# Decay tables by ScalarE's DMA queue, state matmuls on quarter arrays, and tiles that agree modulo 512 bytes, in an attention and two-FFN kernel

## The chip, the core and the metric

One core of one Trainium2 chip runs the whole program. The metric is the device time of one execution in microseconds. The kernel before took 598.75 us (median of 3 runs, 598.46 to 598.89).

## What is computed

Attention with a decay per head, over 2 batches, 8 heads, 768 positions and 64 features a head, then two feed-forward layers on the 1536 tokens (512 to 2048 to 512, the first with x*tanh(softplus(x)), the second with x*clip(x+3,0,6)/6).

```python
Dmask = np.where(rel >= 0, lam[:, None, None] ** rel[None, :, :], 0.0)
intra = np.einsum('bhic,bhjc->bhij', qb, kb) * Dmask[None]
intra = np.einsum('bhij,bhjd->bhid', intra, vb)
inter = np.einsum('bhid,bhde->bhie', qb * lam_pow[None], kv_state)
out[:, :, sl] = intra + inter
kv_state = lam_block * kv_state + np.einsum('bhsd,bhse->bhde', kb * rev_pow[None], vb)
x = moe(attn_out); return moe2(x)
```

## The kernel before

**Attention** works on 12 chunks `c` of 128 positions, 6 for each batch; a chunk holds all 8 heads as 4 pairs `p` of two halves `h2`, with head `2p+h2` on partitions `h2*64` to `h2*64+63`. `load_raw` brings a chunk's q, k, k and v in two halves of 512 KB. `scores` (L148) makes two PSUM tiles `sc`, `weigh` (L163) multiplies them on VectorE by the mask into `amat` (L179) and, in the first four chunks, decays k and q on GpSimd (L170, L172). `attend` (L181) makes `u`, the chunk's addition to the state (L191, only where `carries(c)`), and accumulates in one PSUM bank `o` first 8 matmuls from `amat` (L197), all four pairs of half 0 and then all of half 1, and then, where `follows(c)`, 4 matmuls from `state` (L203). `state` is 128x128 for a pair, with zeros off the diagonal. `settle` (L210) adds `u` to the state on VectorE (L218), splits `o` into a high part on ScalarE and a low part on VectorE in `X`, and scales the state for the next chunk on ScalarE (L226). Of an f32 matmul the profile counts two instructions.

**The two layers** are 96 steps `n` in the list `seq`: each is 12 matmuls `h` (L274) from a weight tile `W[t]` and a token block `X[k]`, and 12 matmuls `y` (L287) from the activation `g` and the same weight tile. The list runs six passes over the upper tiles W8 to W15: one in group "split", two in "add", three in "out"; W0 to W7 have six too.

**Start.** `decay_tables` (L114) loads 8 numbers, makes 128 powers of each on 8 partitions (L126), writes them to DRAM (`z`, L131), and reads them back as the mask (L135) and, spread over all partitions, as `lampow` in `table` (L141). All of its DMAs are on SP's queue, in written order with the loads of `raw` and of the weights' stages `st` around it. The first `h` matmul needs the `X` of chunks 0 to 3, so these come before the layers; chunks 4 to 11 stand between the steps 0 to 15, where `att_at` puts them. Below that, a scheduler orders each engine's instructions.

**Where tiles lie.** Every partition's memory is filled from both ends. From the lower end X, W0 to W11 and g begin at byte 128 modulo 512. From the upper end come the pools tm2 (8192 bytes), tm1 (`pw`, 264 numbers, 1056 bytes), stage, and then at1 and raw; when attention ends, the pool "late" (L488) puts W12 to W15 in the place of the last two. The pools from stage on begin at 448 modulo 512, W12 to W15 among them.

Of the kernel before, what the change touches and what calls it, by code (L numbers as in the profile page):

```python
# [7 lines left out]
F32 = mybir.dt.float32  # L8
# [6 lines left out]
ACTF = mybir.ActivationFunctionType  # L15
ALU = mybir.AluOpType
# [5 lines left out]
def decay_attention__mish_ffn__hswish_ffn_kernel(  # L22
# [8 lines left out]
    nc = tc.nc  # L31
# [10 lines left out]
    tm2_p = ctx.enter_context(tc.tile_pool(name="tm2", bufs=2, side="right"))  # L42
    tm1_p = ctx.enter_context(tc.tile_pool(name="tm1", bufs=1, side="right"))
# [16 lines left out]
    at1 = att_stack.enter_context(tc.tile_pool(name="at1", bufs=1, side="right"))  # L60
# [5 lines left out]
    def split_hi(hi, src):  # L66
        nc.scalar.activation(out=hi, in_=src, func=ACTF.Copy)  # L67

    def split_lo(lo, hi, src):
        nc.vector.tensor_tensor(out=lo, in0=src, in1=f32(hi), op=ALU.subtract)  # L70

    z = dram_p.tile([8, 256], F32, name="z")
    mask = at1.tile([128, 2, 4, 128], F32, name="mask")
    state = [at1.tile([128, 4, 128], F32, name=f"state{i}") for i in range(2)]
    amat = [at1.tile([128, 4, 128], F32, name=f"amat{i}") for i in range(2)]
    table = at1.tile([128, 2, 512], F32, name="table")
    lampow = table[:, 0].rearrange("p (a i) -> p a i", a=4)
# [13 lines left out]
    def load_raw(c, i):  # L91
        if c >= NCH:
            return
        if i == 0:
            pool = lent_p if c in (2, 3) else raw_p
            raw_t[c] = pool.tile([128, 2048], F32, tag="raw", name="raw")
        s = slice(i * 1024, (i + 1) * 1024)
        ins = nc.sync.dma_start(out=raw_t[c][:, s], in_=att[c, :, s])
        if pinned[0]:
            tc.keep_in_program_order(ins)  # L100

    def qk(c):
        t = raw_t[c]
        return (t[:, i:i + 512].rearrange("p (a i) -> p a i", a=4) for i in (512, 0))

    def kv(c):
        t = raw_t[c]
        return t[:, 1024:1536], t[:, 1536:2048]
# [3 lines left out]
        return rr.to_broadcast([128, 4, 2, 64])  # L112

    def decay_tables():  # L114
        lam_sb = tm2_p.tile([128, 512], F32, tag="x", name="lam_sb")[0:8, 0:1]
        pw = tm1_p.tile([128, 264], F32, tag="th", name="pw")[0:8, 0:256]
        nc.sync.dma_start(out=lam_sb, in_=lam.unsqueeze(1))
        load_raw(0, 0)
        load_raw(0, 1)
        load_raw(1, 0)  # L120
        nc.vector.memset(pw[:, 0:127], 0.0)
        nc.vector.memset(pw[:, 127:128], 1.0)
        nc.vector.tensor_copy(pw[:, 128:129], lam_sb)
        m = 1
        while m < 128:
            nc.vector.tensor_scalar(  # L126
                out=pw[:, 128 + m:128 + 2 * m], in0=pw[:, 128:128 + m],
                scalar1=pw[:, 127 + m:128 + m], scalar2=None, op0=ALU.mult,
            )
            m *= 2  # L130
        tc.keep_in_program_order(nc.sync.dma_start(out=z, in_=pw))  # L131
        load_raw(1, 1)
        for h2 in range(2):
            base = z[h2:h2 + 1, 0:1]
            tc.keep_in_program_order(nc.sync.dma_start(  # L135
                out=mask[:, h2],
                in_=bass.AP(base.tensor, base.offset, [[1, 128], [512, 4], [1, 128]]),
            ))
        for h2 in range(2):
            base = z[h2:h2 + 1, 128:129]  # L140
            tc.keep_in_program_order(nc.sync.dma_start(  # L141
                out=lampow[h2 * 64:(h2 + 1) * 64],
                in_=bass.AP(base.tensor, base.offset, [[0, 64], [512, 4], [1, 128]]),
            ))
        for i in range(2):
            nc.gpsimd.memset(state[i], 0.0)

    def scores(c, pool, tag):  # L148
        qT, kT = qk(c)
# [7 lines left out]
    def carries(c):  # L157
        return c % CPB < CPB - 1

    def follows(c):  # L160
        return c % CPB > 0
# [19 lines left out]
    def attend(c, pool, tag):  # L181
        qT, kT = qk(c)
        kn, vn = kv(c)
        u = None
        if carries(c):
            u = ps_a.tile([128, 4, 128], F32, tag="at", name="u")
            for p in range(4):
                for h2 in range(2):
                    s = slice(p * 128 + h2 * 64, p * 128 + h2 * 64 + 64)
                    r = slice(h2 * 64, h2 * 64 + 64)  # L190
                    nc.tensor.matmul(u[r, p, r], lhsT=kn[:, s], rhs=vn[:, s], start=True, stop=True)  # L191
        o = pool.tile([128, 4, 128], F32, tag=tag, name="o")
        last = not follows(c)
        for h2 in range(2):
            for p in range(4):
                h = 2 * p + h2
                nc.tensor.matmul(  # L197
                    o[h2 * 64:h2 * 64 + 64, p, :], lhsT=vn[:, h * 64:h * 64 + 64], rhs=amat[h2][:, p, :],
                    start=(p == 0), stop=(last and p == 3), skip_group_check=True,
                )  # L200
        if follows(c):
            for p in range(4):
                nc.tensor.matmul(  # L203
                    o[:, p, :], lhsT=state[c % 2][:, p, :], rhs=qT[:, p, :],
                    start=False, stop=(p == 3), skip_group_check=True,
                )
        uo_t[c] = u, o
        del raw_t[c]

    def settle(c):  # L210
        u, o = uo_t.pop(c)
        off = (c % 4) * 128
        if carries(c):
            for h2 in range(2):
                r = slice(h2 * 64, h2 * 64 + 64)
                new = state[(c + 1) % 2][r, :, r]
                if follows(c):
                    nc.vector.tensor_tensor(out=new, in0=new, in1=u[r, :, r], op=ALU.add)  # L218
                else:
                    nc.vector.tensor_copy(new, u[r, :, r])  # L220
        hi = X[c // 4][:, 0, :, off:off + 128]
        split_hi(hi, o)
        split_lo(X[c // 4][:, 1, :, off:off + 128], hi, o)
        if carries(c) and carries(c + 1):
            for p in range(4):
                nc.scalar.activation(  # L226
                    out=state[c % 2][:, p, :], in_=state[(c + 1) % 2][:, p, :], func=ACTF.Copy,
                    scale=lampow[:, p, 127:128],
                )

    stage_t = {}

# [170 lines left out]
    nc.scalar.preload_act_table_set("mish")  # L403
    warm_up(10)
    decay_tables()
    load_raw(2, 0)
    load_w(*plan[0])
# [7 lines left out]
    for c in range(4):  # L415
        attend(c, ps_h, "h")
        if c == 0:
            load_raw(4, 0)
            load_w(*plan[2])
            load_raw(4, 1)  # L420
            load_w(*plan[3])
        if c == 1:
            load_raw(5, 0)
            load_raw(5, 1)
            pinned[0] = False
        if c < 3:
            weigh(c + 1)
        else:
            nc.gpsimd.tensor_copy(table[:, 1].rearrange("j (p h d) -> j p h d", p=4, h=2), reverse())
        if c < 2:  # L430
            scores(c + 2, ps_y, "y")
        settle(c)
        if c == 2:
            advance(1)
# [15 lines left out]
    for n in range(STEPS + 2):  # L450
# [12 lines left out]
        for kind in kinds:  # L463
            c = chunk[kind]
            if kind == "s":
                scores(c, ps_a, "at")
                weigh(c)
            else:
                attend(c, ps_a, "at")
                if len(kinds) > 1:  # L470
                    settle(c)
            chunk[kind] += 1
# [7 lines left out]
        if "o" in kinds:  # L480
            c = chunk["o"] - 1
            if len(kinds) == 1:
                settle(c)
            load_raw(c + 2, 0)
            load_raw(c + 2, 1)
            if c == NCH - 1:
                att_stack.close()
                pool = ctx.enter_context(tc.tile_pool(name="late", bufs=1, side="right", reuse_waits="tile"))  # L488
                for i in range(NF - NLATE, NF):
                    W[i] = pool.tile([128, 2, 1024], F32R, name=f"W{i}")  # L490
# [57 lines left out]
```

## Time and profile before

| | |
|---|---|
| median of 3 runs | 598.75 us |
| the profiled execution | 598.68 us |
| its span, first to last instruction | 596.8 us |
| TensorE (PE) busy | 585.1 us, 98% |
| VectorE (DVE) / ScalarE (ACT) busy | 276.6 / 255.9 us |
| PE waits that the profile puts down to another engine or a DMA | 7.8 us |

The profile is of one execution. PE busy is an overlap of pipelined matmuls, so PE's pace is read from the distance between starts: where 12 matmuls of one line are a row of the timeline, the distance to the next row's start is what they took. A "chain" follows the last instruction back through what released it.

### The profile page before, as it was taken

What the parts mean: (1) busy time and instruction counts of PE and PEld (TensorE: products, weight loads), DVE (VectorE), ACT (ScalarE), POOL (GpSimd) and SP (SyncE); (2) the same over time, 40 slices, a digit from 0 to 9 for tenths busy, and PEclk for the clock granted to TensorE, in tenths of its full rate; (3) what the DMA queues carried; (4) which work ended last, traced back from release to release, by engine and by line L of the source; (5) the groups of instructions that cost most, each with busy time, mean ns of one, the idle gap of its engine ahead of it and who ended that gap; (6) DMA issues with size and microseconds to landing.
All of it is one profiled execution on the core that took longest, in us unless ns stands there. A gap on an engine that the chain in (4) does not pass through costs nothing.

```text
span 596.8 us, 7263 instructions
## 1 busy us (share of the span) xinstructions
PE 585.1 (98%) x2938; PEld 477.2 (80%) x2938; DVE 276.6 (46%) x410; ACT 255.9 (43%) x440; POOL 9.7 (2%) x14
## 2 busy tenths in 40 slices
PE   5999999999999999999999999999999999999997
PEld 3877788888888888888888888888888888888885
DVE  2898886733656665510666872222222222222220
ACT  0577767513766666522466652222312222322222
POOL 1400000000000000000000000000000000000000
PEclk9999999999999999999999999999999999999999
DMA  7948744401343343200243220000100000100001
GB/s 228 406 174 290 246 156 142 141 1 71 107 142 116 131 134 113 71 2 0 71 141 113 97 73 1 1 2 0 71 0 1 0 1 0 71 0 1 0 1 70
DMA packets 15952, 50.53 MB, mean 85 GB/s; under 512 B 1576, under 2 KB 3120, under 8 KB 15920
## 3 DMA queue, kind: packets, MB, share of 16 engines
q1 hardware_dynamic: 15920, 50.08, 24.5%
q8 instruction: 23, 0.38, 0.3%
q14 instruction: 9, 0.07, 0.0%
HBM read 46.92 MB, written 3.15 MB: 84 GB/s over the span
## 4 chain that ended last, share of the span: by engine, by line
PE 95%; DVE 2%; DMA 2%; ACT 1%; issue 0%; ACTq 0%; DVEq 0%
PE h L274 44%; PE y L287 44%; PE o L197 3%; PE sc L154 2%; PE o L203 2%; PE u L191 1%; DMA z<-pw 1%; DMA mask<-z 1%; DVE st L255 0%; DVE amat L179 0%; DVE pw L126 0%; DMA lam_sb<-lam 0%; DVE W L70 0%; DVE st L258 0%; ACT W L67 0%
## 5 line engine op out<-in xcount | busy, mean ns | idle before, releaser
L274 PE MATMUL h<-X,W 128*128 128x512 f32 x1152 | 281.4, 393 | 0.0
L274 PEld LDWEIGHTS h<-X,W 128*128 128x128 f32 x1152 | 215.1, 188 | 47.5
L287 PE MATMUL y<-g,W 128*128 128x512 f32 x576 | 139.7, 391 | 0.0
L287 PE MATMUL y<-W,g 128*128 128x512 f32 x576 | 138.9, 391 | 0.0
L287 PEld LDWEIGHTS y<-g,W 128*128 128x128 f32 x576 | 108.0, 188 | 23.8 <-ACT W L67 0.3
L287 PEld LDWEIGHTS y<-W,g 128*128 128x128 f32 x576 | 108.2, 188 | 23.4
L70 DVE TENSOR_TENSOR g<-x,g 128x512 fp32r<-128x512 f32 x96 | 66.2, 691 | 78.9 <-ACT g L310 49.3
L320 DVE SCALAR_TENSOR_TENSOR x<-x,h 128x512 f32<-128x512 f32 x48 | 33.0, 687 | 143.8 <-ACT x L313 143.7
L313 ACT ACTIVATE x<-h 128x512 f32<-128x512 f32 x48 | 28.7, 597 | 144.1 <-PE h L274 144.1
L255 DVE SCALAR_TENSOR_TENSOR st<-st 128x512 int32<-128x512 int32 (+1 forms) x57 | 43.8, 772 | 33.9 <-ACT st L248 33.7
L67 ACT ACTIVATE W<-st 128x512 fp32r<-128x512 f32 (+1 forms) x57 | 41.2, 728 | 32.9 <-DVE st L258 32.5
L309 ACT ACTIVATE x<-h 128x512 f32<-128x512 f32 x48 | 28.6, 596 | 59.7 <-PE h L274 59.6
L247 ACT ACTIVATE st<-st 128x512 f32<-128x512 f32 (+1 forms) x57 | 41.8, 734 | 28.8 <-DMA st<-w 27.2
L70 DVE TENSOR_TENSOR W<-st,W 128x512 fp32r<-128x512 f32 (+1 forms) x57 | 43.3, 765 | 21.6 <-ACT W L67 19.5
L67 ACT ACTIVATE g<-x 128x512 fp32r<-128x512 f32 x48 | 30.3, 632 | 32.2 <-DVE x L320 31.9
L258 DVE SCALAR_TENSOR_TENSOR st<-st 128x512 int32<-128x512 int32 (+1 forms) x57 | 43.1, 757 | 1.5
L248 ACT ACTIVATE st<-st 128x512 int32<-128x512 uint16 (+1 forms) x57 | 41.3, 725 | 0.0
L310 ACT ACTIVATE g<-h 128x512 fp32r<-128x512 f32 x48 | 28.5, 594 | 0.0
L197 PE MATMUL o<-amat,raw 128*64 128x128 f32 x192 | 21.5, 287 | 5.3 <-DVE amat L179 5.2
L197 PEld LDWEIGHTS o<-amat,raw 128*64 128x64 f32 x192 | 17.7, 143 | 7.5 <-DVE amat L179 5.7
L179 DVE TENSOR_TENSOR amat<-sc,mask 128x512 f32<-128x512 f32 x24 | 16.1, 685 | 10.7 <-DMA mask<-z 8.4
L67 ACT ACTIVATE X<-o 128x512 fp32r<-128x512 f32 x12 | 7.1, 593 | 27.6 <-PE o L197 14.9
(34 smaller groups left out, 149.7 us busy)
## 6 DMA issues: line engine op xcount, KB each, us to landing
st<-w SPq DMA_DIRECT2D x50, 512.0 KB, 3.3
raw<-att SPq DMA_DIRECT2D x24, 512.0 KB, 6.1
st<-w SPq DMA_DIRECT2D x7, 1024.0 KB, 6.2
out<-o SPq DMA_DIRECT2D x12, 256.0 KB, 2.0
mask<-z SPq DMA_DIRECT2D x2, 256.0 KB, 3.9
table<-z SPq DMA_DIRECT2D x2, 128.0 KB, 4.2
lam_sb<-lam SPq DMA_DIRECT2D x1, 0.0 KB
z<-pw SPq DMA_DIRECT2D x1, 8.0 KB
```

The lines of the kernel that those rows point to most:

```text
L67: nc.scalar.activation(out=hi, in_=src, func=ACTF.Copy)
L70: nc.vector.tensor_tensor(out=lo, in0=src, in1=f32(hi), op=ALU.subtract)
L197: nc.tensor.matmul(o[h2 * 64:h2 * 64 + 64, p, :], lhsT=vn[:, h * 64:h * 64 + 64], rhs=amat[h2][:, p, :], start=(p == 0), stop=(last and p ...
L247: nc.scalar.activation(out=hf, in_=hf, func=ACTF.Copy, scale=2.0 ** -112)
L248: nc.scalar.activation(out=lo16[..., 0] if sign_on_act else lo, in_=lo16[..., 1], func=ACTF.Copy, scale=2.0 ** -13, bias=2.0 ** -14 - 0.5,)
L255: nc.vector.scalar_tensor_tensor(out=lo, in0=hi, scalar=-2 ** 31, in1=lo, op0=ALU.bitwise_and, op1=ALU.bitwise_or)
L258: nc.vector.scalar_tensor_tensor(out=hi, in0=hi, scalar=3, in1=lo, op0=ALU.logical_shift_left, op1=ALU.bitwise_or)
L274: nc.tensor.matmul(h, lhsT=W[t][:, a, kt * 128:kt * 128 + 128], rhs=X[k][:, b, kt, :], start=(kt, a, b) == order[0], stop=(kt, a, b) == or ...
L287: nc.tensor.matmul(y[e], lhsT=l, rhs=r, start=(first and i == 0), stop=(last and i == 2),)
L309: nc.scalar.activation(out=x, in_=h, func=ACTF.Mish)
L313: nc.scalar.activation(out=x, in_=h, func=ACTF.Relu, bias=3.0)
L320: nc.vector.scalar_tensor_tensor(out=r, in0=r, scalar=6.0, in1=h_t.pop(n), op0=ALU.min, op1=ALU.mult)
```

## The change

The decay tables start from `lam` loaded into all 128 partitions, one DMA for each half, one on SP's queue and one on ScalarE's. The powers are formed there by VectorE directly in `lampow`. The zeros and the one of the mask go to `z` while that runs; then one row of powers from each half goes to `z`, and the mask is read back; all of these DMAs are on ScalarE's queue. SP's queue has only one small DMA ahead of the chunks' loads. `state` keeps only the diagonal: 64 columns for a pair instead of 128, and each state matmul becomes two of 64 rows by 64 columns. The matmuls from `amat` alternate between the halves. VectorE makes the new state in one operation with the scaling, which leaves ScalarE. The tile in tm1 grows from 264 to 344 numbers: 320 bytes, which takes the pools above it, W12 to W15 among them, from 448 to 128 modulo 512.

```diff
-    state = [at1.tile([128, 4, 128], F32, name=f"state{i}") for i in range(2)]
+    state = [at1.tile([128, 4, 64], F32, name=f"state{i}") for i in range(2)]
...
-        pw = tm1_p.tile([128, 264], F32, tag="th", name="pw")[0:8, 0:256]
-        nc.sync.dma_start(out=lam_sb, in_=lam.unsqueeze(1))
-        load_raw(0, 0)
-        load_raw(0, 1)
-        load_raw(1, 0)
...
+        small = tm1_p.tile([128, 344], F32, tag="th", name="small")
+        lam4 = small[:, 0:4].unsqueeze(2)
+        head = small[0:8, 8:136]
+        base = lam[0:1]
+        for h2, queue in ((0, nc.sync), (1, nc.scalar)):
+            tc.keep_in_program_order(queue.dma_start(
+                out=small[h2 * 64:h2 * 64 + 64, 0:4],
+                in_=bass.AP(base.tensor, base.offset + h2, [[0, 64], [2, 4]]),
+            ))
+        nc.vector.memset(head[:, 0:127], 0.0)
+        nc.vector.memset(head[:, 127:128], 1.0)
+        tc.keep_in_program_order(nc.scalar.dma_start(out=z[:, 0:128], in_=head))
+        for c in range(2):
+            load_raw(c, 0)
+            load_raw(c, 1)
+        nc.vector.tensor_copy(lampow[:, :, 0:1], lam4)
         m = 1
         while m < 128:
-            nc.vector.tensor_scalar(
-                out=pw[:, 128 + m:128 + 2 * m], in0=pw[:, 128:128 + m],
-                scalar1=pw[:, 127 + m:128 + m], scalar2=None, op0=ALU.mult,
+            nc.vector.tensor_tensor(
+                out=lampow[:, :, m:2 * m], in0=lampow[:, :, 0:m],
+                in1=lampow[:, :, m - 1:m].to_broadcast([128, 4, m]), op=ALU.mult,
             )
             m *= 2
-        tc.keep_in_program_order(nc.sync.dma_start(out=z, in_=pw))
-        load_raw(1, 1)
+        for h2 in range(2):
+            base = z[h2:h2 + 1, 128:129]
+            tc.keep_in_program_order(nc.scalar.dma_start(
+                out=bass.AP(base.tensor, base.offset, [[0, 1], [512, 4], [1, 128]]),
+                in_=lampow[h2 * 64:h2 * 64 + 1],
+            ))
         for h2 in range(2):
             base = z[h2:h2 + 1, 0:1]
-            tc.keep_in_program_order(nc.sync.dma_start(
+            tc.keep_in_program_order(nc.scalar.dma_start(
                 out=mask[:, h2],
...
-        for i in range(2):
-            nc.gpsimd.memset(state[i], 0.0)
...
-                    nc.tensor.matmul(u[r, p, r], lhsT=kn[:, s], rhs=vn[:, s], start=True, stop=True)
+                    nc.tensor.matmul(u[r, p, 0:64], lhsT=kn[:, s], rhs=vn[:, s], start=True, stop=True)
...
-        for h2 in range(2):
-            for p in range(4):
+        for p in range(4):
+            for h2 in range(2):
                 h = 2 * p + h2
...
-                nc.tensor.matmul(
-                    o[:, p, :], lhsT=state[c % 2][:, p, :], rhs=qT[:, p, :],
-                    start=False, stop=(p == 3), skip_group_check=True,
-                )
+                for h2 in range(2):
+                    r = slice(h2 * 64, h2 * 64 + 64)
+                    nc.tensor.matmul(
+                        o[r, p, :], lhsT=state[c % 2][r, p, :], rhs=qT[r, p, :],
+                        start=False, stop=(p == 3), skip_group_check=True,
+                    )
...
+                for p in range(4):
+                    nc.vector.scalar_tensor_tensor(
+                        out=new[:, p, :], in0=state[c % 2][:, p, :], scalar=lampow[:, p, 127:128],
+                        in1=u[:, p, 0:64], op0=ALU.mult, op1=ALU.add,
+                    )
...
-        if carries(c) and carries(c + 1):
-            for p in range(4):
-                nc.scalar.activation(
-                    out=state[c % 2][:, p, :], in_=state[(c + 1) % 2][:, p, :], func=ACTF.Copy,
-                    scale=lampow[:, p, 127:128],
-                )
```

SP's queue at the start of the program, before (`st` is a stage of weights, `pw` the powers):

```order
L117 DMA lam_sb<-lam 8x1
L98 DMA raw<-att 128x1024 x3
L131 DMA z<-pw 8x256
L98 DMA raw<-att 128x1024
L135 DMA mask<-z 128x4x128 x2
L141 DMA table<-z 64x4x128 x2
L98 DMA raw<-att 128x1024
L236 DMA st<-w 128x512
```

and ScalarE's own stream at the same place now:

```order
L404 ACT_TABLE_LOAD
L120 DMA small<-lam 64x4x1
L126 DMA z<-small 8x128
L140 DMA z<-table 4x1x128 x2
L146 DMA mask<-z 128x4x128 x2
L248 ACTIVATE st<-st 128x512
L249 ACTIVATE st<-st 128x512
L67 ACTIVATE X_81<-o 128x4x128 x2
```

The five DMAs that stood among SP's loads stand behind ScalarE's table load and ahead of its first conversion of weights; SP's loads follow one another.

PE in chunk 4, between the matmuls `h` of step 0, before (the number behind `amat` tells its two halves apart):

```order
L274 MATMUL h<-X_81,W_84 128x512 x17
L191 MATMUL u<-raw 64x64 x8
L197 MATMUL o<-amat_103,raw 64x128 x4
L197 MATMUL o<-amat_104,raw 64x128 x4
L203 MATMUL o<-raw,state_101 128x128 x4
L274 MATMUL h<-X_81,W_84 128x512 x7
```

and now:

```order
L194 MATMUL u<-raw 64x64 x8
L200 MATMUL o<-amat_103,raw 64x128
L200 MATMUL o<-amat_104,raw 64x128
L200 MATMUL o<-amat_103,raw 64x128
L200 MATMUL o<-amat_104,raw 64x128
L200 MATMUL o<-amat_103,raw 64x128
L200 MATMUL o<-amat_104,raw 64x128
L200 MATMUL o<-amat_103,raw 64x128
L200 MATMUL o<-amat_104,raw 64x128
L208 MATMUL o<-raw,state_101 64x128 x8
L275 MATMUL h<-X_81,W_84 128x512 x7
```

The halves alternate, and the four state matmuls are eight. Chunks 8, 9, 10 and 11 have the same pattern (11 without `u`). In chunks 5 and 6 the matmuls from `amat` were cut in two by 12 matmuls `y` and now stand in one piece; in chunk 7 `u` is now parted from them by 6 matmuls `h`.

## Rows read from the trace of the kernel before

**Rows 1.** Waits of PE (engine, line, releaser: total us, times, longest).

```profile
PE o L197 <- DVE amat L179: 5.2, 3, 3.5
```

**Rows 2.** The chain of waits, 0 to 46 us (start us, us, what).

```profile
0.74 1.32 DMA lam_sb<-lam
...
4.04 4.33 DMA z<-pw
...
8.39 3.60 DMA mask<-z
...
31.21 4.12 PE h L274 x17
```

**Rows 3.** Timeline, 0 to 14 us (start us, us, engine, line, operation, shapes).

```profile
0.73 1.28 ACT L403 ACT_TABLE_LOAD   x1 [0.73 <-PEq L540]
...
2.25 1.76 DVE L126 TENSOR_SCALAR pw<-pw 8x1 f32<-8x1 f32 x7
...
13.08 0.69 DVE L179 TENSOR_TENSOR amat<-sc,mask 128x512 f32<-128x512 f32 x1 [0.29 <-DMA mask<-z]
13.15 1.06 POOL L170 TENSOR_TENSOR raw<-raw,mask 128x512 f32<-128x512 f32 x1 [11.44 <-DMA mask<-z]
```

**Rows 4.** Stretches: length, busy us by engine, PEclk, DMA share, GB/s.

```profile
4.00:6.00 2.00, 2.00 (x8) 0.74 (x8) 0.01 (x1) 0.00 (x0) 0.00 (x0) 1.00 0.99 395
10.00:12.00 2.00, 0.00 (x0) 0.00 (x0) 0.00 (x0) 0.00 (x0) 0.00 (x0) 1.00 0.82 208
13.00:16.00 3.00, 3.00 (x28) 2.71 (x29) 1.19 (x3) 0.00 (x0) 2.85 (x4) 0.50 1.03 274
```

**Rows 5.** The page's DMA issues (KB each, median us to landing).

```profile
out<-o SPq DMA_DIRECT2D x12, 256.0 KB, 2.0
```

**Rows 6.** Groups by form on VectorE, whole span (count | busy us, mean ns).

```profile
L255 DVE SCALAR_TENSOR_TENSOR st<-st 128x512 int32<-128x512 int32 x50 | 35.4, 709 | 31.9 <-ACT st L248 31.7
...
L255 DVE SCALAR_TENSOR_TENSOR st<-st 128x1024 int32<-128x1024 int32 x7 | 8.6, 1223 | 2.0 <-ACT st L248 2.0
L218 DVE TENSOR_TENSOR state<-state,u 64x256 f32<-64x256 f32 x16 | 6.7, 416 | 2.5 <-PE u L191 1.8 <-ACT state L226 0.7
```

**Rows 7.** Timeline of PE, chunk 8 and the scores of chunk 9.

```profile
93.89 0.69 PE L191 MATMUL u<-raw 128*64 128x64 f32 x16
94.41 1.53 PE L197 MATMUL o<-amat,raw 128*64 128x128 f32 x16
95.87 1.16 PE L203 MATMUL o<-raw,state 128*128 128x128 f32 x8
96.78 3.00 PE L274 MATMUL h<-X,W 128*128 128x512 f32 x12
99.62 2.88 PE L287 MATMUL y<-g,W 128*128 128x512 f32 x12
102.43 1.16 PE L154 MATMUL sc<-raw 64*128 64x128 f32 x16
103.52 3.02 PE L274 MATMUL h<-X,W 128*128 128x512 f32 x12
106.38 0.84 PE L287 MATMUL y<-g,W 128*128 128x512 f32 x3
```

**Rows 8.** The stretch with chunks 4 to 7 (columns as in rows 4).

```profile
31.00:86.00 55.00, 54.40 (x352) 43.36 (x351) 49.35 (x62) 41.41 (x62) 0.00 (x0) 1.00 0.62 215
```

**Rows 9.** Timeline of PE around the first steps with W12 to W15.

```profile
207.61 2.88 PE L274 MATMUL h<-X,W 128*128 128x512 f32 x12
210.33 2.88 PE L287 MATMUL y<-g,W 128*128 128x512 f32 x12
213.05 2.96 PE L274 MATMUL h<-X,W 128*128 128x512 f32 x12
...
249.19 2.88 PE L287 MATMUL y<-g,W 128*128 128x512 f32 x12
```

**Rows 10.** Groups on PE, by line.

```profile
L203 PE MATMUL o<-raw,state 128*128 128x128 f32 x80 | 11.8, 289 | 0.0
```

More of the change, by code (lines that the diff above doesn't have):

```diff
@@ L114, in decay_tables @@
     def decay_tables():
-        lam_sb = tm2_p.tile([128, 512], F32, tag="x", name="lam_sb")[0:8, 0:1]
-        pw = tm1_p.tile([128, 264], F32, tag="th", name="pw")[0:8, 0:256]
-        nc.sync.dma_start(out=lam_sb, in_=lam.unsqueeze(1))
-        load_raw(0, 0)
-        load_raw(0, 1)
-        load_raw(1, 0)
-        nc.vector.memset(pw[:, 0:127], 0.0)
-        nc.vector.memset(pw[:, 127:128], 1.0)
-        nc.vector.tensor_copy(pw[:, 128:129], lam_sb)
+        small = tm1_p.tile([128, 344], F32, tag="th", name="small")
[14 more added lines that the diff above has]
+        nc.vector.tensor_copy(lampow[:, :, 0:1], lam4)
         m = 1
         while m < 128:
-            nc.vector.tensor_scalar(
-                out=pw[:, 128 + m:128 + 2 * m], in0=pw[:, 128:128 + m],
-                scalar1=pw[:, 127 + m:128 + m], scalar2=None, op0=ALU.mult,
+            nc.vector.tensor_tensor(
+                out=lampow[:, :, m:2 * m], in0=lampow[:, :, 0:m],
+                in1=lampow[:, :, m - 1:m].to_broadcast([128, 4, m]), op=ALU.mult,
             )
             m *= 2
-        tc.keep_in_program_order(nc.sync.dma_start(out=z, in_=pw))
-        load_raw(1, 1)
+        for h2 in range(2):
[4 more added lines that the diff above has]
+            ))
         for h2 in range(2):
             base = z[h2:h2 + 1, 0:1]
-            tc.keep_in_program_order(nc.sync.dma_start(
+            tc.keep_in_program_order(nc.scalar.dma_start(
                 out=mask[:, h2],
@@ L138, in decay_tables @@
             ))
-        for h2 in range(2):
[L140 to L144, printed above, removed]
-        for i in range(2):
-            nc.gpsimd.memset(state[i], 0.0)
     def scores(c, pool, tag):
@@ L190, in attend @@
                     r = slice(h2 * 64, h2 * 64 + 64)
-                    nc.tensor.matmul(u[r, p, r], lhsT=kn[:, s], rhs=vn[:, s], start=True, stop=True)
+                    nc.tensor.matmul(u[r, p, 0:64], lhsT=kn[:, s], rhs=vn[:, s], start=True, stop=True)
         o = pool.tile([128, 4, 128], F32, tag=tag, name="o")
         last = not follows(c)
-        for h2 in range(2):
-            for p in range(4):
+        for p in range(4):
+            for h2 in range(2):
                 h = 2 * p + h2
@@ L213, in settle @@
         if carries(c):
[L214 to L220, printed above, removed]
+            new = state[(c + 1) % 2]
+            if follows(c):
+                for p in range(4):
[3 more added lines that the diff above has]
+                    )
+            else:
+                nc.vector.tensor_copy(new, u[:, :, 0:64])
         hi = X[c // 4][:, 0, :, off:off + 128]
```

## The prediction

> **What bounds the kernel now.** I read the waits first: PE waits for others 7.8 us in the whole span, 5.2 of them for `amat` in the attention at the start [rows 1]. So the kernel has two regions. The first, up to the first `h` matmul at 31.21 us, is a chain that runs through the decay tables [rows 2]. Behind it PE hardly waits for anyone, so there only what PE's instructions themselves take counts, and anything that leaves ScalarE or GpSimd there is worth nothing by itself. The sum is made against the profiled execution, 598.68 us, which is 0.07 us under the median.
>
> In the first region the chain of waits shows `lam` landing after 1.32 us, the powers, then `z`, 4.33 us from issue to landing, then the mask, 3.60 us [rows 2]. `z` is slow for its 8 KB: it stands on SP's queue behind three halves of `raw`, 1.5 MB, and the DMA engines move 395 GB/s at that time [rows 4]. The second half of the mask is there at 13.08 us, when the second `amat` starts and, 0.07 us later, GpSimd's first product [rows 3]. Call this moment M; before, the first `h` is 18.13 us behind M.
>
> In the second region the reader should look at distances between starts. Twelve matmuls `h` or `y` take 2.72 us up to 213.05 us, and from there, where W12 to W15 come in, more: the 13 groups from 213.05 to 249.19 us take 36.14 us, and 13 times 2.72 is 35.36 [rows 9]. W8 to W11, just before, run at 2.72. Nobody is waited for there. What sets W12 to W15 apart is where they lie: at 448 modulo 512, and X, g and all other weights at 128.
>
> **Part 1: tiles at the same place modulo 512.** The 320 bytes added to tm1 put W12 to W15 at 128 too. That it is the place that costs 0.78 us in such a pass isn't shown by an experiment, so the gain lies between nothing and all of it. I take all of it, since W8 to W11 differ from W12 to W15 in nothing else and run at 2.72. There are six passes; the last ends with the kernel and has some 10 of its 13 groups. 5.7 x 0.78 = **4.4 us less**. It falls on PE's own pace, so nothing hides it. It isn't a loss unless W12 to W15 run slower at 128 than at 448, against W0 to W11, which lie there.
>
> **Part 2: attention among the layers (chunks 4 to 11).** The matmuls from `amat`: 16 instructions in 1.46 us now, 94.41 to 95.87 [rows 7]. `u` already alternates between the halves: 16 instructions with half as many columns in 0.52 us. Twice that, 1.04, is one bound; the other is a pair that costs what one full instruction with 128 columns costs, 0.91/8 from the state matmuls, so 0.91 in all. I take 0.95: 0.51 less for a chunk.
>
> The state matmuls: 8 instructions in 0.91 us now, and the 12 `h` behind them take 2.84 (96.78 to 99.62); together 3.75. Sixteen quarter-array instructions have no row. The nearest are the scores, 16 instructions of 64 rows, two at a time: 1.09 us, with 2.86 for the `h` behind them, together 3.95 [rows 7]. So 0.20 more: the shape changes once more on the way back to `h`.
>
> That is 0.31 less for each of chunks 4, 8, 9, 10 and 11, 1.55 in all. Chunks 5 and 6 no longer go into attention twice; one visit costs about 0.3 us beyond its matmuls (1.09 less 0.91, and 2.86 less 2.72, of the scores). Chunk 5 gains 0.31 + 0.3, chunk 6, which has no state matmul, 0.51 + 0.3. In chunk 7 a visit is added, which cancels the gain. The sum is 2.97: **3.0 us less**.
>
> What could take it back is VectorE, busy 49.35 of 55 us in the stretch with chunks 4 to 7 [rows 8]. There its own work grows a little: from 512 and 1024 columns an operation costs 0.20 + 0.0010 a column, so 0.26 for 64 columns [rows 6]; four of them for a state are 1.04 instead of two additions of 0.42. PE's matmuls there could at worst find their gain, some 1.7 us, gone into waits for VectorE; at best they also lose the wait for `amat` in chunk 6, and the gain is 3.9. The four scalings leave ScalarE, and GpSimd's two zero fills leave too: hidden before, worth nothing.
>
> **Part 3: the start.** First M, after the change.
> - `lam`: SP's half lands as before, at 2.06 us. ScalarE's half stands behind its table load, which ends at 2.01 us [rows 3]; whether a DMA issue waits for that, no row tells. Between 2.06 and 3.3 us.
> - Powers: 1.76 + 0.17 us before [rows 3]; now 508 columns in all instead of 127, at 0.0010 a column 0.4 more: 2.4. Done at 4.5 to 5.7 us.
> - `z`: no longer behind `raw` on its own queue. The output's DMAs, to DRAM too, take 2.0 us on quiet queues [rows 5]; the second issue comes some 0.35 later. 6.8 to 8.1 us.
> - Mask: before, 4.69 us from its first issue at 8.39 to M. 11.5 to 12.8 us.
> - But SP doesn't wait for `z` any more. It can send eight halves of `raw` and two stages, 5.2 MB, at once or nearly; at 395 GB/s from 2.4 us on they last until 15.7. If the mask had to wait for all, its own 512 KB at the 208 GB/s of its stretch [rows 4] would end at 18.2.
>
> So M lies between 11.5 and 18.2. I take 14.0, nearer to the queue's own times, since the mask needs a small share of the engines: 0.9 later than now.
>
> Then from M to the first `h`. The order of VectorE decides: `u` of chunk 0 comes 2.2 us behind M (GpSimd's product 1.06 [rows 3], then `u`, about 1.1); the state's copy 0.45, six `amat` at 0.69, two low parts of X at 0.69, seven state operations at 0.26, three operations on weights at 0.71 [rows 6], and eighteen handovers at 0.03: 10.4. Behind the last `amat` stand 0.95 for `o`, 1.09 for the state and 1.09 for the scores of chunk 4. That is 15.7; I add 0.4 because weights' operations beside GpSimd are slower: 16.1, against 18.13. The gain has three sources: chunk 1's product for q on GpSimd now needs only `lampow` and comes before M; ScalarE's scalings leave the chain; and `o` is shorter. PE's clock was at the lower of its two levels, 0.50, from 13 to 16 us, after two microseconds and more without a matmul [rows 4]; it idles about as long in the change, so I count nothing.
>
> The first `h` stands at 14.0 + 16.1 = 30.1: **1.1 us less** than 31.21.
>
> **Sum.** 598.68 - 4.4 - 3.0 - 1.1 = 590.2 us. Behind chunk 11 the order of PE is the same.
>
> **Rivals.**
> 1. *The mask comes last.* SP's loads crowd it out: M at 18.2, the first `h` at 34.3, and 594.4 us. For it: both queues are served by the same engines, busy 0.99 at the start [rows 4]; against it: a mask on its own queue doesn't stand behind the loads. The Trainium skill (DMA: Bandwidth & Descriptors, section "Issuing engines are not separate DMA queues") says that DMAs of different issuers run on the same 16 engines and interleave, and that issuing from several saves only the issue time; by that the result is this rival's. The rows here show one queue alone and can't tell.
> 2. *The place doesn't matter.* Parts 2 and 3 alone: 594.6 us. Against it is only that W8 to W11 run at 2.72.
> 3. *The two row halves of a state matmul don't run together*, slower than before at its worst. Both now write the same PSUM bank `o`; the scores, which do run two at a time, write two banks. If each of the 16 took a full turn, 0.114 us, the 8 chunks on the path (7 among the layers, and chunk 3) would cost 128 x 0.057 = 7.3 us more: 597.5. If each had to pass through the array before the next starts, 0.289 [rows 10], it is 128 x 0.232 = 29.7 more: 620 us. From 0.123 an instruction on (8.5 us over 128, on top of 0.057) the change is slower. For it: no row has two row halves in one bank. Against it: `u` writes one bank from two column halves and runs two at a time. The Trainium skill (TensorEngine Tiling (Array Packing), section "Restrictions and Gotchas") says that different row tiles cannot access the same PSUM bank at once; by that rule this rival happens.
> 4. *VectorE becomes the bound in chunks 4 to 7*: 1.7 us of part 2 lost, 591.9, inside the forecast's own range.
>
> **How the numbers follow.** A measurement of this kernel can tell about 0.2%, 1.2 us. The forecast with its bounds, 587 to 593, has 0.70, rival 4 among it; rival 1 has 0.12, rival 2 0.08, rival 3 0.07 (half of it slower, half near 597.5), and 0.03 are left for what I don't see. Faster: 0.70 + 0.12 + 0.08 and a little, 0.91; the same 0.04; slower 0.05. The range reaches down to all three parts at their best (4.4 + 3.9, and M at 11.5 with 15.7 behind it, 4.0: 586.4; I take 586.8) and up through rivals 1 and 2 to 594.8.
>
> **What would show it.** Part 1: `h` and `y` with W12 to W15 at 2.72 a group; at 2.75 to 2.80 it is wrong. Part 2: 16 instructions from `amat` in about 0.95 us, and 16 state instructions in about 1.1; near 1.8 or 4.6 rival 3 is right. Part 3: the second `amat` at about 14 us and the first `h` at about 30; the mask landing over 8 us after its issue is rival 1. A new wait of PE for VectorE between 30 and 85 us is rival 4. A first `h` later than 34 us would make the prediction of part 3 wrong in kind.

## The result, and the profile after

The changed kernel took **606.24 us** (median of 4 runs, 605.29 to 608.01) against 598.82 us for the kernel before on the same chip: a ratio of 1.013, 95% interval 1.0108 to 1.0153. It is slower by 7.4 us, where 590.2 us, 8.5 faster, was forecast. The profiled execution took 606.7 us, its span is 604.9 us.

The chain of waits of the changed kernel, 0 to 46 us (start us, us, what), answers to [rows 2]:

```profile
0.77 9.37 DMA small<-lam
...
12.32 4.04 DMA z<-table
...
16.46 9.21 DMA mask<-z
...
25.76 0.70 DVE amat L182
...
44.36 1.81 PE h L275 x7
```

The first `h` is 13.15 us later than before (44.36 against 31.21). Step by step: `lam` is there at 10.13 instead of 2.06 us, 8.1 later. Powers and `z` take what they took: `lam` to the first mask issue, 6.33 us before (2.06 to 8.39), is again 6.33. The moment M of the prediction is read by GpSimd's first product, in the timeline:

```profile
26.51 2.07 POOL L173 TENSOR_TENSOR raw<-raw,mask 128x512 f32<-128x512 f32 x2 [9.27 <-DMA mask<-z]
```

From the mask's first issue to it: 10.05 us (16.46 to 26.51) instead of 4.76 (8.39 to 13.15 [rows 3]), 5.3 more. From there to the first `h`: 17.85 instead of 18.06.

Stretches of the changed kernel (columns as in [rows 4]) show what the DMA engines did:

```profile
2.00:4.00 2.00, 2.00 (x6) 0.76 (x5) 0.00 (x0) 0.01 (x1) 0.00 (x0) 1.00 0.04 0
4.00:6.00 2.00, 1.49 (x4) 0.30 (x2) 0.00 (x0) 0.00 (x0) 0.00 (x0) 1.00 0.04 0
6.00:8.00 2.00, 0.00 (x0) 0.00 (x0) 0.00 (x0) 0.00 (x0) 0.00 (x0) 1.00 0.38 112
...
20.00:22.00 2.00, 0.00 (x0) 0.00 (x0) 0.00 (x0) 0.00 (x0) 0.00 (x0) 0.50 0.97 373
22.00:24.00 2.00, 0.00 (x0) 0.00 (x0) 0.00 (x0) 0.00 (x0) 0.00 (x0) 0.50 1.02 365
24.00:26.00 2.00, 0.00 (x0) 0.00 (x0) 0.24 (x1) 0.00 (x0) 0.00 (x0) 0.50 0.31 94
...
30.00:32.00 2.00, 2.00 (x18) 1.67 (x15) 1.98 (x4) 0.60 (x1) 0.15 (x1) 0.50 0.03 8
```

Between 4 and 6 us they moved 395 GB/s before and nothing now, though SP has issued the raw loads from 1.54 us on; and from 20 to 26 us, while the mask is read, 1.66 MB pass (2 us each of 373, 365 and 94 GB/s), of which the whole mask is 0.5. The DMA view of 0 to 12 us (line, engine, KB each, median us from issue to landing) has the `raw` loads as late as `lam`:

```profile
raw<-att SPq DMA_DIRECT2D x5, 512.0 KB, 9.9
...
small<-lam ACTq DMA_DIRECT2D x1, 1.0 KB, 9.4
```

PE waits accordingly; the view of waits, whole span, in place of [rows 1]:

```profile
PE o L200 <- DVE amat L182: 11.4, 3, 10.7
PE sc L157 <- DMA raw<-att: 6.5, 2, 6.0
...
PE h L275 <- DVE W L70: 0.7, 1, 0.7
PE sc L157 <- DVE state L227: 0.6, 1, 0.6
PE u L194 <- DVE raw L180: 0.6, 1, 0.6
PE y L288 <- DVE W L70: 0.3, 1, 0.3
```

Behind the first `h` the kernel is faster. Chunk 8 on PE's timeline, against [rows 7]:

```profile
107.81 0.69 PE L194 MATMUL u<-raw 128*64 128x64 f32 x16
108.32 1.05 PE L200 MATMUL o<-amat,raw 128*64 128x128 f32 x16
109.30 1.09 PE L208 MATMUL o<-raw,state 64*64 64x128 f32 x16
110.32 3.02 PE L275 MATMUL h<-X,W 128*128 128x512 f32 x12
113.17 2.88 PE L288 MATMUL y<-g,W 128*128 128x512 f32 x12
```

From `u` to `h` it is 2.51 us (2.89 before). And where W12 to W15 come in, against [rows 9], the groups keep their pace, 17 from 211.93 to 258.17 us in 46.24 us, 2.72 each:

```profile
211.93 2.88 PE L288 MATMUL y<-g,W 128*128 128x512 f32 x12
214.65 2.88 PE L275 MATMUL h<-X,W 128*128 128x512 f32 x12
...
258.17 2.88 PE L275 MATMUL h<-X,W 128*128 128x512 f32 x12
```

So 13.15 us were lost up to the first `h` and 5.1 gained behind it (first `h` to last matmul: 561.46 before, 556.38 now), 8.0 between the profiled executions.

### The profile page after: what moved, and what is told of

The parts are those of the page before. It is cut to its first block, busy times and chain, and to the rows that moved or that the text cites. A ratio compares the mean times of both kernels' runs of the same rounds, so it can differ in the third digit from the quotient of the medians.

```text
span 604.9 us, 7403 instructions
## 1 busy us (share of the span) xinstructions
PE 579.7 (96%) x3018; PEld 473.5 (78%) x3018; DVE 274.3 (45%) x424; ACT 246.9 (41%) x408; POOL 8.7 (1%) x12
## 4 chain that ended last, share of the span: by engine, by line
PE 88%; DMA 6%; DVE 3%; ACT 1%; issue 1%; ACTq 0%; DVEq 0%
PE h L275 42%; PE y L288 41%; DMA st<-w 2%; PE o L200 2%; DMA small<-lam 2%; DMA mask<-z 2%; PE sc L157 1%; PE o L208 1%; PE u L194 1%; DMA z<-table 1%; DVE W L70 1%; DVE st L259 1%; DVE st L256 1%; ACT st L249 0%; DVE amat L182 0%
## 5 line engine op out<-in xcount | busy, mean ns | idle before, releaser
L70 DVE TENSOR_TENSOR W<-st,W 128x512 fp32r<-128x512 f32 (+1 forms) x57 | 42.9, 755 | 18.2 <-ACT W L67 16.7
L157 PE MATMUL sc<-raw 64*128 64x128 f32 x192 | 18.9, 320 | 7.1 <-DMA raw<-att 6.5
L200 PE MATMUL o<-amat,raw 128*64 128x128 f32 x192 | 14.7, 288 | 11.4 <-DVE amat L182 11.4
L157 PEld LDWEIGHTS sc<-raw 64*128 64x128 f32 x192 | 16.0, 218 | 12.1 <-DMA raw<-att 7.5
```

Of the source, the lines that this page charges most:

```text
L157: nc.tensor.matmul(sc[h2][:, p, :], lhsT=kT[r, p, :], rhs=qT[r, p, :], start=True, stop=True)
```

## The experiments

Each kernel was timed against the kernel before on the same chip (598.6 to 598.84 us). "First `h`" is its first start in PE's timeline: 31.14 us before, 44.29 in the changed kernel.

| run | us | ratio, interval | first `h` |
|---|---|---|---|
| e1, place alone | 594.00 | 0.9904 to 0.9934 | 30.97 |
| e2, matmuls and state alone | 596.06 | 0.9925 to 0.9965 | 29.64 |
| e3, both | 591.21 | 0.9852 to 0.9889 | 28.88 |
| e4, `lam` as 128 packets of 32 B | 598.90 | 0.9990 to 1.0016 | 38.89 |
| e5, 512 packets, 512 places | 600.08 | 1.0016 to 1.0040 | 37.68 |
| e9, all `lam` on ScalarE's queue | 608.31 | 1.0095 to 1.0172 | 44.70 |
| e12, 512 packets, one other place | 605.05 | 1.0090 to 1.0129 | 43.32 |
| e6, e3 with z, mask on ScalarE's queue | 595.32 | 0.9924 to 0.9954 | 35.39 |
| e7, e6 without SP's loads beside | 594.50 | 0.9913 to 0.9943 | 34.05 |
| e10, e3 and 512 unused packets, one place | 596.20 | 0.9940 to 0.9970 | 34.37 |
| e11, the same, 512 places | 592.71 | 0.9887 to 0.9927 | 31.05 |
| e8, e3 with the mask early | 593.54 | 0.9904 to 0.9972 | 30.26 |

### What each part is worth: e1, e2, e3, e4

e1 is the kernel before with

```diff
-        pw = tm1_p.tile([128, 264], F32, tag="th", name="pw")[0:8, 0:256]
+        pw = tm1_p.tile([128, 344], F32, tag="th", name="pw")[0:8, 0:256]
```

> The kernel before with one number changed: the tile in tm1 has 344 numbers in place of 264, so W12 to W15 move from 448 to 128 modulo 512. If the place sets the pace of the matmuls that use them, all groups of 12 take 2.72 us and the time is 4.4 us less than before: 594.4. If the place does not matter, 598.8.

4.7 us less. Over the whole run the distances between the starts of neighbouring matmuls `h` and `y` (those under 240 ns; longer ones are waits) exceed 226.7 ns by 0.33 us in sum, against 4.74 before: the place of the tiles alone is the cause. Only this one shift of 320 bytes was tried, so that the remainder by 512 decides, and not another property of the place, isn't shown.

e2 is the changed kernel with the tables and the tile of 264 numbers of the kernel before; e3 has the tables of before and the tile of 344.

> The state of 64 columns, the quarter-array state matmuls, the alternating halves and the state's update in one operation, all of them on the kernel before, with its decay tables and its place of the tiles. Theory: 3.0 us less among the layers and 1 to 2 us less between the mask's landing and the first h, 594 to 596. Rival (the quarter-array matmuls of one bank exclude each other): 597.5 or more.

> Place and matmuls of the change together, with the decay tables of the kernel before. If all of the loss comes from the new tables, 590 to 592, faster than both kernels. If something else in the change costs time (VectorE's state operations, the shorter state), above 594.

Against the kernel before on their chip (598.67 us) e2 gains 2.6 us and e3 7.5; the two parts add up within 0.2, and **e3 beats both kernels**. The chain of e3:

```profile
4.07 4.18 DMA z<-pw
...
8.69 3.98 DMA mask<-z
...
12.84 1.07 POOL raw L168
...
28.95 3.17 PE h L270 x13
```

With the tables on SP's queue as before, GpSimd's first product stands at 12.84 us and the first `h` 16.1 behind it. So all of the loss, 606.24 - 591.21 = 15.0 us, is in the new way to the tables. e4 loads all 8 numbers to each partition in one load on ScalarE's queue, 128 packets of 32 B instead of 512 of 4.

```diff
-        for h2, queue in ((0, nc.sync), (1, nc.scalar)):
-            tc.keep_in_program_order(queue.dma_start(
-                out=small[h2 * 64:h2 * 64 + 64, 0:4],
-                in_=bass.AP(base.tensor, base.offset + h2, [[0, 64], [2, 4]]),
-            ))
+        lam8 = small[:, 136:144]
+        tc.keep_in_program_order(nc.scalar.dma_start(
+            out=lam8, in_=bass.AP(base.tensor, base.offset, [[0, 128], [1, 8]]),
+        ))
...
```

> The changed kernel, but lam comes as one DMA on ScalarE's queue, 128 rows of 32 bytes (8 packets for each DMA engine), and not as two DMAs of 256 elements of 4 bytes (16 packets for each engine, one DMA on each queue). If packets of 4 bytes that follow each other at about 0.24 us on an engine are the cause, lam lands at 3 to 5 us, the first raw at about 6 us and not 11.4, and the time is 5 to 7 us less than the changed kernel's: 599 to 601. If the loads are slow for another reason (ScalarE's queue, both halves reading the same few bytes of DRAM), lam lands at 8 us or later and the time stays above 604.

```profile
0.76 5.85 DMA small<-lam
...
12.75 8.96 DMA mask<-z
```

`lam` lands 3.5 us earlier (6.6 us), between my two forecasts for it, the time falls by 7.3 us, yet the mask still takes 9.0 us. Two costs, then: the load of `lam`, and z and mask on the second queue.

### The load of lam: e5, e9, e12

e5 changes only where the 512 packets read: 256 places for each of the two loads, 512 in all, at least 512 bytes apart.

```diff
-                in_=bass.AP(base.tensor, base.offset + h2, [[0, 64], [2, 4]]),
+                in_=att[0, h2 * 64:h2 * 64 + 64, 0:512].rearrange("p (a n) -> p a n", a=4)[:, :, 0],
```

> The changed kernel, but its two loads of four numbers for each of 64 partitions read 256 different places of att instead of the same 8 numbers of lam, with as many packets of 4 B (the powers are then of numbers of att, not of lam). Theory (what holds the start up is the number of 4-byte packets, some 0.24 us each on a DMA engine, with the raw loads behind them): small still lands at 9 to 11 us, the first gemm at 43 to 46 us, time 604 to 608 us. Rival (all packets read the same 32 bytes of DRAM and queue there): small lands before 6 us, the first gemm comes at 37 to 40 us, time 598 to 602 us.

e9 has `((0, nc.scalar), (1, nc.scalar))` in place of `((0, nc.sync), (1, nc.scalar))`.

> The changed kernel with both loads of lam on ScalarE's queue, so that nothing stands ahead of the raw loads on SyncE's. Theory (512 packets of 4 B take their time wherever they are queued, and those on SyncE's queue held the raws): the raws' packets begin by 3 us and the first raw lands at 5.5 to 8 us, but small lands as late as before or later, 9 to 14 us, since all its packets now share one queue beside the raws; z and mask 3.5 to 4.5 and 8.5 to 9.5 us as in the changed kernel; first gemm at 42 to 48 us, time 604 to 610 us. Rival (it was SyncE's queue that was slow, its start or its half of the packets): small lands by 7 us, first gemm by 40 us, time below 601 us.

The chain of e5, then that of e9:

```profile
0.77 3.25 DMA small<-att
```

```profile
1.57 9.80 DMA small<-lam
```

My theory, the number of packets, fell with e5: as many packets land in 3.25 us when they read different places, and the rival's time came. e9 shows that the queue isn't it either: `lam` is no earlier (11.37 us), the first `raw` is early (its scores start at 5.45 us), and then the stream stops, though nothing stands ahead of it on SP's queue any more:

```profile
2.00:4.00 2.00, 2.00 (x6) 0.76 (x5) 0.00 (x0) 0.01 (x1) 0.00 (x0) 1.00 0.85 234
4.00:6.00 2.00, 2.00 (x13) 0.86 (x13) 0.00 (x0) 0.00 (x0) 0.00 (x0) 1.00 0.13 35
```

e5 mixed two things, other places and another tensor. e12 parts them, with `base = att[0, 0:1, 0:1]` in place of `base = lam[0:1]`:

> The changed kernel with its two loads of 512 packets of 4 B reading one and the same 8 numbers of att, its first ones, and not lam's (the powers are then of numbers of att). With the run that read 256 different places of att it tells apart what was mixed there: one place, or the tensor lam itself. Theory (many reads of one place, whichever it is): small lands at 9 to 11 us, the raws are held as in the changed kernel, first h at 43 to 46 us, time 604 to 608 us. Rival (it is lam's own place in memory that is slow): small lands by 4.5 us, first h at 37 to 39 us, time 599 to 602 us.

```profile
0.77 8.86 DMA small<-att
```

It is one place read by 512 packets, whichever tensor it lies in: 8.86 us, 0 GB/s from 2 to 6 us as in the changed kernel.

### Who is held by it: e10, e11

Both are e3 with two loads more, whose result nothing reads; e10 reads the 8 numbers of `lam`, e11 the places of `att` that e5 reads.

```diff
+        for h2 in range(2):
+            tc.keep_in_program_order(nc.scalar.dma_start(
+                out=extra[h2 * 64:h2 * 64 + 64],
+                in_=bass.AP(base.tensor, base.offset + h2, [[0, 64], [2, 4]]),
+            ))
```

> The version with the tables of before and the new row length and matmuls (591.2 us) plus the changed kernel's two loads of lam (512 packets of 4 B that read the same 32 bytes), both issued by ScalarE's queue into columns that nothing reads, so that nobody waits for them. Theory (reads of one place hold up other transfers too): the raw loads' bytes between 4 and 8 us fall to less than half of 395 GB/s, z and mask land 3 to 6 us later (mask at 15.5 to 18.5 us), time 594 to 598 us. Rival (only what waits for the small packets is late): mask at 12.5 to 13.5 us, time 591 to 592.5 us.

> As the run before, but the two extra loads read 256 different places of att, in as many packets of 4 B; nothing reads what they load. Theory (it is the one place, not the number of packets): raw loads at 350 GB/s or more between 4 and 8 us, mask at 12.5 to 14 us, time 591 to 592.5 us. Rival (512 small packets cost the engines their time wherever they read): mask at 15 us or later, time 594 us or more.

The DMA view of 0 to 10 us, of e10 and of e11:

```profile
raw<-att SPq DMA_DIRECT2D x4, 512.0 KB, 9.6
pw<-lam ACTq DMA_DIRECT2D x2, 1.0 KB, 8.4
```

```profile
raw<-att SPq DMA_DIRECT2D x4, 512.0 KB, 5.8
...
pw<-att ACTq DMA_DIRECT2D x2, 1.0 KB, 3.6
```

The stretch from 4 to 6 us of e3, of e10 and of e11 (columns as in [rows 4]):

```profile
4.00:6.00 2.00, 1.95 (x18) 1.08 (x18) 0.04 (x1) 0.00 (x0) 0.00 (x0) 1.00 0.99 389
4.00:6.00 2.00, 1.64 (x4) 0.30 (x2) 0.15 (x1) 0.00 (x0) 0.00 (x0) 1.00 0.28 105
4.00:6.00 2.00, 1.24 (x8) 0.52 (x8) 0.02 (x1) 0.00 (x0) 0.00 (x0) 1.00 0.70 216
```

Nobody waits for these packets, and still e10's `raw` loads take 9.6 us (4.8 in e3), `z` 7.69, and the time is 5.0 us above e3. In e11 it is 1.5 above: GpSimd's first product stands at 14.25 us, a little later than I had put it, and from 4 to 6 us the engines moved 216 GB/s where I had put 350 or more. So reads of one place hold up other transfers, and 512 small packets from as many places do so too, but less, and for a shorter time.

### z and the mask beside SP's stream: e6, e7

e6 is e3 with z, mask and table issued by `nc.scalar` (`lam` and the powers as before). In e7 the loads of chunks 2 and 3 and the first two of weights follow on that queue too:

```diff
-        ins = nc.sync.dma_start(out=raw_t[c][:, s], in_=att[c, :, s])
+        ins = (nc.scalar if c in (2, 3) else nc.sync).dma_start(out=raw_t[c][:, s], in_=att[c, :, s])
...
```

> Powers and tables in the form before the change (lam as 8 packets of 4 B, ahead of the raws on SyncE's queue, powers on 8 partitions), row length and matmuls of the changed kernel; only the loads and stores z, mask and table issued by ScalarE's queue. Theory (beside SyncE's stream of raw loads and weights a transfer on ScalarE's queue gets a share and takes twice as long): z 3.5 to 4.5 us, mask 8 to 9.5 us, the mask lands at 16 to 18 us instead of 12.7, first gemm at 32 to 34 us, time 594 to 596 us, against 591.2 us with all of it on SyncE's queue. Rival (the move to ScalarE's queue is harmless or gains, all the loss was the load of lam): z 2.4 us, mask 4 to 5 us, mask at 11 to 12 us, first gemm at 27 to 28.5 us, time 589 to 591 us.

> As the run before, but the raw loads of chunks 2 and 3 and the first two loads of weights are also issued by ScalarE's queue, behind the tables, so that nothing is left on SyncE's queue while the mask is read. Theory (the mask's 9 us are contention with SyncE's loads, not the queue itself): z still some 4 us beside the raws of chunks 0 and 1, mask 3.5 to 5 us, it lands at 11 to 13.5 us, first gemm at 27.5 to 30 us, time 589 to 593 us (the loads of chunks 2 and 3 start some 6 us later, which may cost up to 1 us). Rival (a transfer of 512-byte packets that ScalarE issues is slow by itself): mask 8 to 9 us, it lands at 16 us or later, time 594 us or more.

The chain of e6, then of e7:

```profile
4.04 5.96 DMA z<-pw
...
10.50 7.84 DMA mask<-z
...
18.41 1.07 POOL raw L168
```

```profile
4.05 5.33 DMA z<-pw
...
9.84 4.59 DMA mask<-z
...
14.59 1.07 POOL raw L168
...
19.98 12.41 DMA st<-w
```

Beside SP's loads the mask takes 7.84 us, twice e3's 3.98, and `z` 5.96; `z`, the mask's landing and the first `h` come later than I had put them, the time is as forecast. With no load of SP's beside it the mask on the same queue takes 4.59. So it is contention, not the queue. e7's time was still 594.5: its mask lands 1 us later than I had put it, since `z` is slow beside chunks 0 and 1, and the postponed weights then land at 32.4 us and hold the first `h`. What the mask gained, the weights lost.

### A better order: e8

e8 is e3 with SP's order `lam`, `raw` (0,0), `z`, `raw` (1,0), mask, and only then `raw` (0,1) and (1,1), each as (chunk, half).

> The version with the tables of before and the new row length and matmuls (591.2 us), everything on SyncE's queue, in another order there: lam, raw of chunk 0 (first half), z, raw of chunk 1 (first half), the two mask loads, then the other two halves, then the tables; so z and mask stand behind 0.5 MB each and not behind 1.5 MB. Theory (in the queue's order what stands ahead is the price): z issued at 4.04 us and landed by 6 to 7 us, mask landed at 10 to 11.5 us instead of 12.7, first gemm at 26 to 28 us instead of 28.9, time 588.5 to 590.5 us. Rival (the time after the first gemm is set by the raws and weights, which stay as many): first gemm earlier but the time 590.5 to 592 us.

`z` takes 1.30 us there and the mask is there at 10.1 us, but the rest of `raw` lands at 12.3, and its chain runs over that: the first `h` comes 1.4 us later than in e3. The median, 593.54 us, lies above both forecasts. Its ten runs spread from 591.4 to 599.7 us; the four above 597 have a mean granted clock of 0.982 to 0.985, the others 0.991 to 0.994. What sets the one or the other wasn't tried. e3 stays the best.

## Why the prediction was wrong

**The step that failed is the start, part 3**, and in it first the term "`lam`: ... Between 2.06 and 3.3 us". By the prediction's own sign, a first `h` later than 34 us, part 3 was wrong in kind. I had asked only whether ScalarE's table load delays the issue. It doesn't, as two rows of the timeline of the changed kernel show:

```profile
0.73 1.28 ACT L404 ACT_TABLE_LOAD   x1 [0.73 <-PEq L541]
...
0.77 0.76 ACTq L120 DMA_DIRECT2D small<-lam  x1
```

I costed the DMA itself, 256 packets of 4 B a queue from 8 numbers, by the old load of 8 packets, whose 1.32 us was the nearest row for the issue but not for what is read. It landed at 10.13. e5 and e12 show why: 512 reads of one place.

The same reads held the `raw` loads, and this I hadn't in any rival. With the numbers of e5 it is 606.24 - 600.08 = 6.2 us of the loss.

**z: "6.8 to 8.1 us", so 2.35 from the powers' end.** It took 4.04 in the changed kernel and 5.96 in e6. "No longer behind `raw` on its own queue" was true and worth next to nothing (4.33 before): `z` went beside the same 512 KB loads. **The mask: "4.69 us from its first issue"** to M took 10.0. I had its upper bound, M at 18.2, as rival 1 with a chance of 0.12, and took 14.0 "since the mask needs a small share of the engines". e6, which has this step without the load of `lam`, has M at 18.41: rival 1's own place. The rule that spoke for it, in the Trainium skill (DMA: Bandwidth & Descriptors, section "Issuing engines are not separate DMA queues"), agrees with e6 and e7: 7.84 us beside SP's loads, 4.59 without. This step costs 595.32 - 591.21 = 4.1 us.

**The sum of the loss:** e3 to e6 4.1 us, e6 to e5 4.8, e5 to the changed kernel 6.2, together 15.0. The middle one is the load of 512 packets, powers on all partitions and zeros sent ahead; of it, 2.3 us show in the first `h` (35.39 to 37.68), where `lam` lands 2.0 us later. Behind 30 us PE waits 2.8 us for others in e5 and 1.0 in e6. And in e5's profiled execution, the longest of its ten (602.95 us), PE's granted clock is at its lower level, 0.50, once more among the layers, from 73.8 to 80.7 us; whether other runs of e5 have this too, no trace shows. One stretch of it:

```profile
76.00:80.00 4.00, 4.00 (x14) 3.29 (x14) 4.00 (x5) 1.61 (x4) 0.00 (x0) 0.50 0.44 123
```

**From M to the first `h`, 16.1 us.** e3 has 16.1 (12.84 to 28.95), in part by luck: chunk 1's product for q, which the forecast has ahead of M, still comes behind it there (15.42 us). In the changed kernel that product does come ahead (15.97 us), and the way takes 17.85; the chain there runs through conversions of weights on VectorE, which it doesn't in e3. For PE's clock I counted nothing. The granted clock was at 0.50, the lower level, up to 32.5 us, 6.0 us past GpSimd's first product, and before up to 16.1 us, 2.9 past it; in e3 up to 5.3 past it. What that costs wasn't separated.

**Part 1** (4.4 us) was right: 4.7 in e1, and 0.40 us of excess left in the changed kernel.

**Part 2** (3.0 us) was right in mechanism, and its size shows only where PE waits little. `o` takes 0.98 us (0.95 forecast), and from the state matmuls' start to 12 `h` later it is 3.87 us (109.30 to 113.17), 3.95 forecast. But of e2's gain 1.5 us come ahead of the first `h` (29.64 for 31.14). From there to the last matmul e2 takes 560.55 us for 561.46 before, and e3 556.00 for e1's 556.98: 0.9 and 1.0 less, not 3.0. Behind 30 us PE waits for others 0.5 us before, 1.9 in e2 and 2.1 in e3; in e3 most of it is:

```profile
PE sc L152 <- DVE state L222: 0.9, 1, 0.9
PE y L283 <- ACT W L67: 0.9, 1, 0.9
```

In e4 and e6, with the first `h` at 38.89 and 35.39, the waits are 0.9 and 1.0 us, and the same way takes 553.84 and 553.96 us: the forecast's 3 us less than e1. So the loss that rival 4 names, 1.7 us of part 2, came about in e2 and e3. The wait in the first line is for a copy into `state`, which the kernel before has too, and the second for a weight's conversion on ScalarE; whether VectorE's new operations or the order of the conversions bring them about wasn't tried. In the changed kernel the waits of PE for VectorE are 2.2 us, some for weights and some for `state` and k: the last four rows of the view of waits. That e3 met its forecast, 590 to 592 us, is luck in part: the start gave 2.3 us, for 1 to 2 expected, and the layers 1.0 for 3.0.

**Rival 2** falls with e1. **Rival 3** falls: 16 instructions from `state` take 1.02 us (109.30 to 110.32), 0.064 each, and not 0.114 or 0.289; the scores, which write two banks, take 1.09 (115.99 to 117.08). The Trainium skill (TensorEngine Tiling (Array Packing), section "Restrictions and Gotchas") has it that row tiles can't access the same PSUM bank at once. The two halves that write different partitions of the bank `o` ran at this pace here, so the measurement decides against the rule.

By the terms: the first `h` is 14.2 us later than forecast (44.3 against 30.1; M alone 12.5), and the way from there to the last matmul is 2.3 us longer than forecast (556.38 against 561.46 less 7.4), about what PE waits for VectorE there; that makes the 16.5 us between 590.2 and the profiled 606.7. The range missed because the load of `lam` had a lower end from a row and an upper end from a question, the table load, that wasn't its own: a transfer unlike every row of the trace, 512 packets from one place instead of 8, needed an upper end as far off as its count of packets, and a rival of its own.

## What to carry to other kernels

A load that spreads a few numbers over all partitions is many reads of one place: here 8 packets to 8 partitions landed in 1.3 us and 512 in 9.4, and the second kind held the loads beside it. Before a transfer that the start waits for is moved to a second queue, list what the first queue is then free to send, and price the transfer beside that. Where a change has parts that can be had apart, cost them apart: two of these were worth 7.5 us, and the third lost 15.0.

## What the runs showed of the hardware

- 512 packets of 4 B that read the same 32 bytes took 8.4 to 9.8 us, of `lam` or of `att`, from one queue or two; from 512 places 3.25 to 3.6 us. During the former, loads on another queue that read elsewhere fell to 35 GB/s (e9, 4 to 6 us) and 105 GB/s (e10); beside the latter they moved 216 (e11), and 389 without either (e3). 128 packets of 32 B from one place took 5.85 us (e4), 8 packets of 4 B 1.32 us. What in the memory makes it so wasn't tried.
- In the chain the mask took 3.98 us in its turn on SP's queue (e3), 7.84 on a second queue beside SP's loads (e6), 4.59 there without SP's loads (e7).
- Matmuls `h` and `y` whose weights lie at 448 modulo 512 while X and g lie at 128 run 2.2% slower than with all at 128 (36.14 us for 35.36, [rows 9]); 320 bytes of padding gave back 4.7 us of 599. No other shift was tried.
- ScalarE issued a DMA at 0.77 us, while its table load ran (0.73 to 2.01 us).
